# Low parts of decoded weights: ScalarE writes the negated high part and an accumulating GpSimd transfer adds the decoded block, in place of a VectorE subtraction

## Chip, cores and metric

The kernel runs on one core of one Trainium2 chip. The metric is device time in microseconds. Each execution of a kernel gives one time, and the median over the executions is compared. One more execution is recorded by the hardware profiler; its span, its groups of instructions and its waits are what this text reads.

## What is computed

Sink-and-window attention for 4 batches and 8 heads of 768 tokens, followed by a feed-forward block on the joined heads. The two matrices of the feed-forward block arrive as 64-bit floats, read as pairs of 32-bit words.

```python
def _attn_ref(q, k, v, n_sink, window):
    scores = np.matmul(q, k.transpose(0, 1, 3, 2)) / np.sqrt(64)
    keep = is_sink | in_window            # first 4 keys, or the last 128
    a = softmax(np.where(keep, scores, -1e9))
    return np.matmul(a, v)                # (4, 8, 768, 64)

def _moe_ref(x, w_in, w_out):             # x: 3072 x 512, w_in: 512 x 2048
    h = x @ w_in
    g = np.where(h >= 1, h, np.where(h <= -1, 0.0, (h + 1) ** 2 / 4))
    return g @ w_out
```

## The kernel before

**Two parts for every operand.** TensorE multiplies fp32r operands, which keep fewer bits than fp32. So an operand is written as a high part (its value rounded to fp32r) and a low part (the value less the high part), and each product is three matmuls: high by high, high by low, low by high. `w_i[j]` and `w_o[j]` hold both parts of block `j` of the two weight matrices, `t[:, 0]` the high and `t[:, 1]` the low one, each 128 x 512. There are 16 blocks of each matrix, so 32 blocks to decode, numbered `n` = 0 to 31, alternating between `w_in` and `w_out`.

**Decoding.** `weights(n)` loads the raw words of block `n` and of up to three blocks ahead (512 KB each, tile `raw`, shown as `w<-w_in` and `w<-w_out`, the first eight from SyncE's queue and the rest from ScalarE's) and calls `decode`. Three VectorE instructions (L153, L154, L155) shift and join the two words into the fp32 value in the scratch tile `w` (128 x 512). ScalarE rounds it into `t[:, 0]` (L156), and VectorE subtracts that from the value into `t[:, 1]` (L157). The scratch tile is called `o` in the profile, because it comes from a pool of two buffers under that name (pool `moe`, `bufs=2`); block `n` therefore writes the buffer that block `n-2` used.

**Stages.** 64 units of attention (a batch, a head and half the tokens, three score tiles each) form eight chunks of eight units. Beside chunk 0 stand the first 6 decode steps. Beside chunk 1 stand decode steps 6 to 27 and the first half of the feed-forward for chunk 0's rows (blocks 0 to 7). Beside chunk 2 stand the last four decode steps and the whole feed-forward of the next rows. After that no weights are decoded. Each score tile has one L243 on VectorE (mask and row maximum), whose exponential is L246 on ScalarE; each unit has one L251 on GpSimd and one L252 on VectorE, which prepare the normalisation (L264 on ScalarE and L266 on VectorE in the first 16 units). Tiles are counted by their L243: tile 12 ends unit 4, tile 36 ends unit 12 and tile 60 ends unit 20. In the profiled execution their L243 start at 22.42, 67.54 and 127.90 us.

**Order.** TensorE's order is the order of the program text (`spread` interleaves the steps by their weights). On the other engines a scheduler orders the instructions, so an added or removed instruction can move others. Each engine and each queue runs its instructions in the order given; an instruction that waits holds everything behind it on its engine.

Of the kernel before, what the change touches and what calls it, by code (L numbers as in the profile page):

```python
# [8 lines left out]
F32 = mybir.dt.float32  # L9
# [3 lines left out]
AF = mybir.ActivationFunctionType  # L13
ALU = mybir.AluOpType
# [38 lines left out]
def attn_ffn(ctx, tc, qk, vx, vs, par, w_in, w_out, out):  # L53
    nc = tc.nc
# [96 lines left out]
    def decode(t, w, words):  # L151
        low, x = words[:, :, 0], words[:, :, 1]
        nc.vector.tensor_scalar(w, x, 3, 0x3FFFFFFF, op0=ALU.logical_shift_left, op1=ALU.bitwise_and)  # L153
        nc.vector.scalar_tensor_tensor(w, x, -0x40000000, w, op0=ALU.bitwise_and, op1=ALU.bitwise_or)  # L154
        nc.vector.scalar_tensor_tensor(w, low, 29, w, op0=ALU.logical_shift_right, op1=ALU.bitwise_or)  # L155
        nc.scalar.copy(t[:, 0], w.bitcast(F32))  # L156
        nc.vector.tensor_tensor(t[:, 1], w.bitcast(F32), t[:, 0].bitcast(F32), op=ALU.subtract)  # L157

    top = {}

    def weights(n):
        def f():
            j, i = n // 2, n % 2
            for k in range(n, min(n + min(AHEAD, NJ - n // 2 - 1) + 1, 2 * NJ)):
                if k not in raw:
                    raw[k] = wpool.tile([P, 2 * DM], I32, name="w")
                    (nc.sync if k < SYNC else nc.scalar).dma_start(raw[k], (w_in, w_out)[k % 2][k // 2].bitcast(I32))
            words = raw[n].rearrange("p (c two) -> p c two", two=2)
            if i:
                w_o[j] = wpool.tile([P, 2, DM], F32R, name="w")  # L170
            decode((w_i, w_o)[i][j], moe.tile([P, DM], I32, name="o"), words)
        return f
# [440 lines left out]
    with tc.If(other_v > 0):  # L613
        with tc.tile_pool(name="gen", bufs=1) as gen:

            for n in range(2 * NJ):
                words = gen.tile([P, DM, 2], I32, name="words")
                nc.sync.dma_start(words.rearrange("p c two -> p (c two)"), (w_in, w_out)[n % 2][n // 2].bitcast(I32))
                xf = words[:, :, 1].bitcast(F32)
                m = gen.tile([P, DM], F32, name="m")  # L620
                nc.vector.tensor_tensor(m, xf, xf, op=ALU.mult)
                nc.vector.scalar_tensor_tensor(xf, m, TINY2, xf, op0=ALU.is_ge, op1=ALU.mult)
                decode((w_i, w_o)[n % 2][n // 2], m.bitcast(I32), words)
            for t0 in (0, CT):
                keep = gen.tile([P, CT, S], F32, name="keep")
                kidx = gen.tile([P, S], I32, name="kidx")
                r = gen.tile([P, S], F32, name="r")
                for i in range(CT):
                    m = keep[:, i]
                    nc.gpsimd.iota(kidx, pattern=[[-1, S]], base=(t0 + i) * P, channel_multiplier=1)  # L630
                    nc.vector.tensor_copy(r, kidx)
                    nc.vector.tensor_scalar(m, r, w_f, None, op0=ALU.is_lt)
                    nc.vector.scalar_tensor_tensor(m, r, 0.0, m, op0=ALU.is_ge, op1=ALU.mult)
                    nc.gpsimd.iota(kidx, pattern=[[1, S]], base=0, channel_multiplier=0)
                    nc.vector.tensor_copy(r, kidx)
                    nc.vector.scalar_tensor_tensor(m, r, n_f, m, op0=ALU.is_lt, op1=ALU.max)
                    nc.vector.tensor_scalar(m, m, 0.125, None, op0=ALU.mult)
                for b in range(B):
                    for h in range(H):
                        general(gen, keep, b, h, t0)  # L640
                    tail = []
                    for _, f in moe_steps(b * S + t0 * P, tail) + tail:
                        f()
# [37 lines left out]
```

## Time and profile before

| | before |
|---|---|
| median of 3 runs | 736.66 us (735.27 to 738.84) |
| profiled execution | 737.31 us, span 735.5 us, mean granted clock 0.988 |
| TensorE matmuls | 696.8 us busy (95%) |
| VectorE | 528.7 us (72%) |
| ScalarE | 507.0 us (69%) |
| GpSimd | 307.2 us (42%) |
| DMA moved | 77.79 MB, mean 106 GB/s |

The profiled execution lasted 737.31 us, which is 0.65 us over the median; it is 1.8 us longer than its span. The shares are averages over two different stages. Up to about 150 us weights are loaded and decoded beside the attention of the first chunks. After that only attention and the feed-forward remain. A row with a line number names the source line; `o<-w,o` means that a tile named `o` is written from tiles named `w` and `o`. PE is TensorE, DVE is VectorE, ACT is ScalarE, POOL is GpSimd and SP is SyncE.

### The profile page before, as it was taken

Reading aid. Unit: us, or ns where it says so; the run is one execution under the profiler, and the core shown is the slowest. Engines: PE = TensorE matmul, PEld = TensorE weight load, DVE = VectorE, ACT = ScalarE, POOL = GpSimd, SP = SyncE. Lnnn points to the kernel's source line nnn. Section 1 sums busy time; section 2 is a strip of 40 time slices with the busy share of each in tenths; the row PEclk is TensorE's granted clock in tenths of the full one; section 3 lists DMA queues with packets and bytes.
Section 4 is the critical chain, followed back from the end, with each engine's and each line's share of the span. In section 5 each row is a group of like instructions: output and inputs, shape, how many; then the busy total and the mean of one; then the engine's idle time right before and its main releaser. Section 6 shows DMA issues by size and latency. Waiting matters only on the chain.

```text
span 735.5 us, 12356 instructions
## 1 busy us (share of the span) xinstructions
PE 696.8 (95%) x3841; PEld 615.7 (84%) x3841; DVE 528.7 (72%) x1396; ACT 507.0 (69%) x1313; POOL 307.2 (42%) x537
## 2 busy tenths in 40 slices
PE   5669889899999999999999999999999999999996
PEld 3337678789999999999979998899889999989995
DVE  8999996987655666568777887877887777742221
ACT  4888797776576665578767876778767776645342
POOL 3112166554346434236554555645666454500000
PEclk9989999999999999999999999999999999999998
DMA  8987543312131311134423542324334342101001
GB/s 268 327 268 255 170 115 96 99 46 54 42 100 45 100 40 58 34 119 128 124 81 117 156 121 85 116 73 156 124 114 119 103 131 85 66 2 44 0 1 47
DMA packets 48265, 77.79 MB, mean 106 GB/s; under 512 B 13632, under 2 KB 32064, under 8 KB 48192
## 3 DMA queue, kind: packets, MB, share of 16 engines
q1 hardware_dynamic: 44736, 64.34, 28.9%
q10 hardware_dynamic: 3456, 12.58, 4.8%
q8 instruction: 32, 0.52, 0.3%
q14 instruction: 41, 0.34, 0.2%
HBM read 69.83 MB, written 7.08 MB: 105 GB/s over the span
## 4 chain that ended last, share of the span: by engine, by line
PE 64%; DVE 17%; ACT 7%; DMA 7%; issue 2%; POOL 2%; SPq 0%; ACTq 0%; POOLq 0%; DVEq 0%
PE o_ps L458 28%; PE h_ps L439 27%; PE ps_a L402 4%; DMA w<-w_in 4%; PE ps_a L239 3%; ACT p L246 2%; DVE p L266 2%; DVE k_s L223 1%; DVE o L154 1%; PE ps_a L334 1%; DVE o L155 1%; DVE p L258 1%; DVE gl L450 1%; DVE p L243 1%; DVE o L153 1%
## 5 line engine op out<-in xcount | busy, mean ns | idle before, releaser
L439 PE MATMUL h_ps<-x,wi 128*128 128x384 f32 x1536 | 308.7, 340 | 0.4 <-DVE x L480 0.4
L439 PEld LDWEIGHTS h_ps<-x,wi 128*128 128x128 f32 x1536 | 263.5, 188 | 9.3 <-DVE x L480 0.7
L458 PE MATMUL o_ps<-w,gh 128*128 128x512 f32 x768 | 244.6, 399 | 0.0
L458 PE MATMUL o_ps<-w,gl 128*128 128x512 f32 x384 | 151.3, 394 | 0.0
L458 PEld LDWEIGHTS o_ps<-w,gh 128*128 128x128 f32 x768 | 135.2, 189 | 15.7 <-issue 0.3
L446 ACT ACTIVATE g<-h_ps,half 128x384 f32<-128x384 f32 x128 | 73.9, 578 | 69.7 <-PE h_ps L439 67.7
L448 DVE SCALAR_TENSOR_TENSOR g<-g,h_ps 128x384 f32<-128x384 f32 x128 | 70.2, 549 | 68.6 <-ACT g L447 68.0
L246 ACT ACTIVATE p<-p,peak 128x260 f32<-128x260 f32 (+1 forms) x192 | 93.9, 489 | 33.9 <-DVE peak L243 32.0
L225 POOL TENSOR_TENSOR q_l<-r,q_h 128x384 fp32r<-128x384 f32 x48 | 50.3, 1047 | 142.5 <-ACT q_h L224 141.6
L449 ACT CAST gh<-g 128x384 fp32r<-128x384 f32 x128 | 65.5, 512 | 56.9 <-DVE g L448 55.9
L243 DVE CUSTOM_DVE_ANT_0 p<-ps_a,m 128x260 f32<-128x260 f32 (+1 forms) x176 | 68.5, 398 | 31.8 <-PE ps_a L239 30.5
L239 PE MATMUL ps_a<-k_s,q_h 128*128 128x260 f32 (+1 forms) x240 | 71.2, 345 | 18.6 <-DMA k_s<-qk 6.1
L458 PEld LDWEIGHTS o_ps<-w,gl 128*128 128x128 f32 x384 | 72.3, 188 | 17.5
L450 DVE TENSOR_TENSOR gl<-g,gh 128x384 fp32r<-128x384 f32 x112 | 68.0, 607 | 24.5 <-ACT gh L449 23.6
L223 DVE TENSOR_TENSOR k_s<-k_r,k_s 64x524 fp32r<-64x524 f32 (+1 forms) x44 | 45.4, 1032 | 40.9 <-ACT k_s L221 40.9
L239 PEld LDWEIGHTS ps_a<-k_s,q_h 128*128 128x128 f32 x240 | 45.2, 203 | 33.3 <-issue 10.9
L447 ACT ACTIVATE g<-g 128x384 f32<-128x384 f32 x128 | 67.0, 523 | 2.7
L346 POOL TENSOR_SCALAR_AFFINE_SELECT pt<-pt 128x384 fp32r<-128x384 f32 (+1 forms) x96 | 50.8, 530 | 24.2 <-DVE pt L339 21.7
L266 DVE TENSOR_SCALAR p<-p,stat 128x132 f32<-128x132 f32 (+1 forms) x160 | 59.1, 418 | 0.3
L344 POOL TENSOR_SCALAR_AFFINE_SELECT pt<-pt 128x384 fp32r<-128x384 f32 (+1 forms) x96 | 52.5, 547 | 8.9 <-ACT pt L338 3.9
L251 POOL TENSOR_SCALAR stat<-stat 128x3 f32<-128x3 f32 x64 | 28.6, 447 | 62.2 <-ACT p L246 53.8
L402 PEld LDWEIGHTS ps_a<-pt,v_s 128*128 128x128 f32 x304 | 46.5, 189 | 2.0
(117 smaller groups left out, 955.3 us busy)
## 6 DMA issues: line engine op xcount, KB each, us to landing
r<-qk SPq DMA_DIRECT2D x48, 192.0 KB
k_r<-qk SPq DMA_DIRECT2D x32, 262.0 KB
again<-w_in SPq DMA_DIRECT2D x16, 512.0 KB
again<-w_out SPq DMA_DIRECT2D x16, 512.0 KB
w<-w_in ACTq DMA_DIRECT2D x12, 512.0 KB
w<-w_out ACTq DMA_DIRECT2D x12, 512.0 KB
out<-o SPq DMA_DIRECT2D x23, 256.0 KB
r<-vx SPq DMA_DIRECT2D x32, 128.0 KB
```

Source lines behind the costliest of these rows:

```text
L239: nc.tensor.matmul(ps[:, lo:260], lhsT=q[:, i * P:(i + 1) * P], rhs=k_s[:, c0:c0 + 260 - lo], start=(j == 0), stop=(j == len(qs) - 1))
L243: nc.vector.tensor_tensor_reduce(out=p[:, i, lo:260], in0=ps[:, lo:260], in1=m, scale=-0.0625 if units.index(u) < NATIVE else -0.125, scal ...
L246: nc.scalar.activation(p[:, i, lo:260], p[:, i, lo:260], AF.Exp, bias=peak_i, scale=-1.0, accum_out=stat[:, i:i + 1])
L266: (nc.gpsimd if eng == "p" else nc.vector).tensor_scalar(p[:, i, lo:260], p[:, i, lo:260], r, None, op0=ALU.mult)
L402: nc.tensor.matmul(z, lhsT=w, rhs=y, start=(n == 0), stop=(n == len(mms) - 1))
L439: nc.tensor.matmul(h_ps[:, :T], lhsT=w_i[j][:, w, ct * P:(ct + 1) * P], rhs=x[:, y, ct], start=(ct == 0 and n == 0), stop=(ct == NCT - 1 a ...
L446: nc.scalar.activation(g, h_ps[:, :T], AF.Relu, bias=half, scale=0.5)
L447: nc.scalar.activation(g, g, AF.Square)
L448: nc.vector.scalar_tensor_tensor(g, g, 1.0, h_ps[:, :T], op0=ALU.min, op1=ALU.max)
L449: nc.scalar.copy(gh, g)
L450: (nc.gpsimd if row0 == GL_POOL else nc.vector).tensor_tensor(gl, g, gh.bitcast(F32), op=ALU.subtract)
L458: nc.tensor.matmul(o_ps[tt], lhsT=gg[:, tt * P:(tt + 1) * P], rhs=w_o[j][:, w], start=(j == js[0] and n == 0), stop=(j == js[-1] and n == 2))
```

## The change

The subtraction on VectorE is replaced by two steps. ScalarE writes the negated high part into `t[:, 1]`: it copies the value times -1 with the same rounding. Then a transfer issued from GpSimd's queue reads the fp32 value from the scratch tile and adds it onto `t[:, 1]` in place, which leaves the value less its high part.

```diff
         nc.scalar.copy(t[:, 0], w.bitcast(F32))
-        nc.vector.tensor_tensor(t[:, 1], w.bitcast(F32), t[:, 0].bitcast(F32), op=ALU.subtract)
+        nc.scalar.activation(t[:, 1], w.bitcast(F32), AF.Copy, scale=-1.0)
+        nc.gpsimd.dma_start(t[:, 1].bitcast(F32), w.bitcast(F32), accum_op=ALU.add)
```

Below line 157 all line numbers of the changed kernel are one higher: L243 becomes L244, L251 becomes L252. TensorE's order in the part that runs here is the same in both kernels. On VectorE the scheduler moves the decode steps. The first excerpt is from VectorE just after blocks 0 and 1 have been put together, in the kernel before; the numbers behind the names tell buffers apart (`o_358` belongs to block 2, `o_442` to block 3).

```order
L252 RECIPROCAL stat_232<-stat_232 128x3
L157 TENSOR_TENSOR wi0_151<-o_204,wi0_151 128x512
L266 TENSOR_SCALAR p_231<-p_231,stat_232 128x128
L153 TENSOR_SCALAR o_358<-w_200 128x512
L157 TENSOR_TENSOR w_289<-o_290,w_289 128x512
L154 SCALAR_TENSOR_TENSOR o_358<-w_200,o_358 128x512
L243 ISA p_268,peak_97<-ps_a_270,m0_109 128x128
```

Block 2 starts ahead of unit 3's first tile (the last row), two rows after block 0's buffer was last read. In the changed kernel block 2 (`o_360`) starts after all three tiles of units 3 and 4, directly ahead of block 3 (`o_445`), and each L153 waits for the transfer that reads the buffer's earlier content; this is VectorE again, at that later place.

```order
L244 ISA p_317,peak_97<-ps_a_327,m2_106 128x260
L253 RECIPROCAL stat_318<-stat_318 128x3
L267 TENSOR_SCALAR p_317<-p_317,stat_318 128x128
L153 TENSOR_SCALAR o_360<-w_200 128x512
L154 SCALAR_TENSOR_TENSOR o_360<-w_200,o_360 128x512
L153 TENSOR_SCALAR o_445<-w_202 128x512
L155 SCALAR_TENSOR_TENSOR o_360<-w_200,o_360 128x512
L481 TENSOR_TENSOR x0_181<-xn_169,x0_181 128x384
L154 SCALAR_TENSOR_TENSOR o_445<-w_202,o_445 128x512
```

What moved is the whole decoding: the L153 of block 2 from behind tile 6 to behind tile 12, that of block 13 from behind tile 24 to behind tile 36, and that of block 27 from behind tile 46 to behind tile 60. On GpSimd, which had no transfer of its own, the changed kernel has one between the normalisation steps for each block; these are its rows at blocks 0 to 2.

```order
L252 TENSOR_SCALAR stat_233<-stat_233 128x3
L158 DMA wi0_151<-o_204 128x512
L158 DMA w_290<-o_291 128x512
L252 TENSOR_SCALAR stat_270<-stat_270 128x3
L252 TENSOR_SCALAR stat_318<-stat_318 128x3
L284 MEMSET v_s_407 128x128
L299 TENSOR_TENSOR vsx0_137<-vs_r_1343,vsx0_137 44x64
L158 DMA wi1_152<-o_360 128x512
```

Each of these transfers stands ahead of the next unit's L252, which VectorE's reciprocal needs.

## Prediction

> **What bounds the kernel now.** I read the stages first, cut at the places the order names: tiles 12, 36 and 60 (22.4, 67.5 and 128 us). The columns are busy time of each engine, the granted clock of TensorE, and the share of the 16 DMA engines in use.
>
> ```profile
> core 0: us, PE busy (x) PEld busy (x) DVE busy (x) ACT busy (x) POOL busy (x), PEclk, DMA share, GB/s
> 9.00:22.40 13.40, 9.73 (x33) 5.42 (x34) 13.28 (x43) 10.78 (x35) 1.49 (x3) 1.00 0.97 308
> 22.40:67.50 45.10, 34.90 (x188) 22.75 (x186) 44.05 (x129) 38.27 (x116) 4.88 (x14) 0.89 0.83 282
> 67.50:128.00 60.50, 55.69 (x326) 45.90 (x325) 52.53 (x137) 49.48 (x141) 30.04 (x41) 0.97 0.46 140
> 128.00:150.00 22.00, 18.43 (x103) 15.69 (x102) 21.48 (x51) 14.24 (x40) 11.36 (x18) 1.00 0.32 91
> 150.00:300.00 150.00, 150.00 (x841) 137.45 (x841) 96.70 (x270) 101.08 (x262) 66.26 (x117) 1.00 0.21 60
> ```
>
> From 150 us TensorE is busy without a break and the change touches nothing there. So the change is worth what it does ahead of 150 us, and since TensorE's order is unchanged, each microsecond by which tile 60 comes later or earlier passes to the end. Until tile 36 VectorE is full (44.05 of 45.10 us), with ScalarE at 85% and the DMA engines at 83 to 97%. From tile 36 to 60 TensorE leads (55.69 of 60.50).
>
> Next the groups of the decode steps, and the chain that ended last, with the spacing of instructions on VectorE and the landings of weight loads (start, length, what; a DMA piece runs from its issue to its landing).
>
> ```profile
> L155 DVE SCALAR_TENSOR_TENSOR o<-w,o 128x512 int32<-128x512 int32 x32 | 23.7, 741 | 0.1
> L154 DVE SCALAR_TENSOR_TENSOR o<-w,o 128x512 int32<-128x512 int32 x32 | 23.2, 725 | 0.2
> L153 DVE TENSOR_SCALAR o<-w 128x512 int32<-128x512 int32 x32 | 14.7, 460 | 0.7 <-DVE stat L252 0.3 <-DMA w<-w_in 0.2
> L157 DVE TENSOR_TENSOR w<-o,w 128x512 fp32r<-128x512 f32 x16 | 11.8, 737 | 0.9 <-ACT w L156 0.9
> L157 DVE TENSOR_TENSOR wi<-o,wi 128x512 fp32r<-128x512 f32 x16 | 11.8, 736 | 0.0
> L156 ACT CAST w<-o 128x512 fp32r<-128x512 f32 x16 | 9.8, 614 | 1.6 <-DVE o L155 1.4
> L156 ACT CAST wi<-o 128x512 fp32r<-128x512 f32 x16 | 9.8, 611 | 6.3 <-DVE o L155 6.3
> ```
>
> ```profile
> 4.07 7.47 DMA w<-w_in
> ...
> 14.94 0.34 DVE o L153
> ...
> 17.03 0.60 DVE o L155
> 17.63 0.34 DVE p L243
> ...
> 17.97 0.60 DVE o L154
> ...
> 18.92 0.60 DVE wi L157
> ...
> 20.55 6.94 DMA w<-w_in
> ```
>
> ```profile
> 33.11 4.06 DMA w<-w_in
> ...
> 62.45 5.08 DMA w<-w_in
> ```
>
> ```profile
> 122.49 1.02 POOL q_l L225
> ...
> 125.48 2.02 DMA part<-o
> ...
> 138.02 3.44 DMA w<-w_out
> ```
>
> The reader sees that one L157 holds VectorE for 0.60 us, that a 512 KB load lands after 6.9 to 7.5 us while the DMA engines are 97% busy, after 4.1 to 5.1 us at 83%, and after 3.4 us when they are at a third.
>
> **Removed.** 32 x 0.60 = 19.2 us of VectorE. Of these 14 run between tiles 12 and 36; there 14 x 0.60 = 8.4 us go, and since four blocks less are decoded in that stretch afterwards (11 instead of 15), another 4 x (0.34 + 0.60 + 0.60) = 6.2 us. VectorE falls from 44.05 to about 29.5 us of that stage and is no bound there any more.
>
> **Added on ScalarE.** 32 copies of the size of L156. The two following rows show what one holds the engine for: the next instruction starts 0.50 us later.
>
> ```profile
> 13.30 0.60 ACT L156 CAST wi<-o 128x512 fp32r<-128x512 f32 x1
> 13.80 0.36 ACT L327 COPY pt<-ps_a 128x256 f32<-128x256 f32 x1
> ```
>
> I take 0.53 us each (between that spacing and the 0.61 of its length), 17 us in all. Between tiles 12 and 36: 38.27 - 15 x 0.53 + 11 x 2 x 0.53 = 42.0 us. Between 36 and 60 (10 casts now, 13 blocks later): 49.48 - 5.3 + 13.8 = 58.0 us. These are floors, since ScalarE would have to run without a pause. So VectorE's relief cannot be worth more than 45.1 - 42.0 = 3.1 us and 60.5 - 58.0 = 2.5 us in these stages. Ahead of tile 12, blocks 2 and 3 leave VectorE, and ScalarE's 10.78 us would bound it: at most 13.40 - 10.78 = 2.6 us. From 128 to 150 us, where VectorE is full (21.48 of 22 us), three L157 go, 1.8 us. Together 10.0 us is the most that can be won.
>
> **Added on GpSimd and the DMA engines.** 32 transfers, each reading a 256 KB block and the 256 KB it is added to. GpSimd is idle for most of this time (4.88 of 45.10 us), but a transfer waits there for its negated copy, and L251 of the next unit stands behind it, and behind that the reciprocal on VectorE. The trace has neither a transfer from GpSimd nor an accumulating one. From below: 2.0 us, the 256 KB `part<-o` with half-idle engines. From above: 7.5 us, the 512 KB load ahead of tile 12, with 1.05 us for GpSimd's issue (as long as one L225, 1.02) where SyncE's costs 0.43 of the load's time: 8.1 us. Two rows are near: traffic of 512 KB is that of a weight load, so I take the loads' landings of the same stage. For tiles 12 to 36 the rows are 6.94, 4.06 and 5.08, at a DMA share of 0.83. The transfers raise that share: 11 x 0.5 MB = 5.8 MB at 282 GB/s / 0.83 = 340 GB/s are 17 us of 45, or half of that if only the block itself counts, 0.19 to 0.38 more. The engines are then as full as ahead of tile 12, so I take that stage's rows, 7.2 us (7.47 and 6.94). For tiles 36 to 60, 14 transfers bring 0.46 to about 0.8; there 4.06 and 5.08 apply, 4.6 us.
>
> The Trainium skill, "DMA: Bandwidth & Descriptors", section on the anatomy of a transfer from GpSimd, fits one as 2.0 us plus its bytes over 436 GB/s, an estimate of 2.6 us for 256 KB and 3.2 us for 512 KB. The 2.02 us row agrees, the 6.94 us row of the busy stage doesn't; by it the transfer would be hidden, which is the first rival's case.
>
> **The wait that it makes.** Before, a scratch buffer was free when L157 had read it, and L153 of block n+2 never waited for it. Now it is free when the transfer of block n has landed, and that L153 stands on VectorE with the attention's rows behind it. One turn of a buffer: L153, L154, L155 with about one tile's row between them, 0.34 + 0.60 + 0.60 + 0.4 = 2.0 us (rounded up); 0.5 us until ScalarE takes it up (the rows below: L155 ends its hold at 23.37, L156 starts at 24.17; in other places 0.1); cast and negated copy 0.50 + 0.61 = 1.1 us; then the transfer, T. That is 3.6 us + T for two blocks.
>
> ```profile
> 22.77 0.68 DVE L155 SCALAR_TENSOR_TENSOR o<-w,o 128x512 int32<-128x512 int32 x1
> 23.37 0.42 DVE L153 TENSOR_SCALAR o<-w 128x512 int32<-128x512 int32 x1
> ```
>
> ```profile
> 24.17 0.60 ACT L156 CAST wi<-o 128x512 fp32r<-128x512 f32 x1
> ```
>
> What the places in the order allow: blocks 2 to 13 lie between tiles 12 and 36, 11 steps in 45.1 us, 4.1 us each, a turn of 8.2 us, so T up to 4.6 us is hidden. Blocks 13 to 27 lie between tiles 36 and 60, 14 steps in 60.5 us, a turn of 8.6 us, T up to 5.0 us. The first is exceeded: 3.6 + 7.2 = 10.8 us a turn, 5.4 us a block, 11 x 5.4 = 59.4 us where 45.1 stood, +14.3 us. The second is not: 3.6 + 4.6 = 8.2 us. Ahead of tile 12 block 2's buffer is awaited from about 14.4 (both copies of block 0) + 7.2 = 21.6 us, just before tile 12, so little is won there. The matmuls themselves don't wait for weights: their blocks 0 to 7 are used beside decode steps 6 to 27.
>
> **Sum.** On the profiled execution of 737.3 us: -19.2 us of VectorE, of which nothing ends up at the end because the waits take its place, +17 us of ScalarE beside those waits, +14.3 us of waiting between tiles 12 and 36, 0 after tile 36. That gives 751.6 us; the median of the runs is 0.65 us below that execution, so 751 us.
>
> Ends of the range. Below, T is hidden everywhere and ScalarE runs without a pause: 737.3 - 10.0 = 727. Above, T = 8.1 us everywhere: a turn of 11.7 us, 11 x 5.85 - 45.1 = +19.3 us and 14 x 5.85 - 60.5 = +21.4 us, 778 us.
>
> **Rivals.**
> (1) The transfer is hidden, T below 4.6 us throughout. For it: GpSimd is idle, nothing reads HBM in these transfers, and the 2.02 us and 3.44 us rows. Against it: 83 to 97% busy DMA engines. VectorE's relief then counts, limited by ScalarE. It was 80 to 85% busy in its best stages and would have to be 93 to 96% busy; I give half the floors' gain, 5 us: 732 us.
> (2) Gains and losses cancel: T between about 4.6 and 5.5 us early, so that 11 x (3.6 + 5.5) / 2 = 50 us costs 5 us, against up to 5 us won ahead of tile 12 and after tile 36. 737 us, within 0.5% of before. That is about the least change that a measurement of this kernel can tell from none.
> (3) The transfer is slower than any row: GpSimd is held from building it. L153 (128 x 512 in 0.42 us) runs faster than L154 (0.68 us), so VectorE works there in another mode. The Trainium skill, "SBUF — State Buffer", in its box on SBUF's two sides, says that GpSimd cannot write a transfer's descriptors while VectorE runs in a mode that takes both ports; no transfer here can show it yet. Were each transfer held for one L153, 0.42 us, that adds 0.2 us to each of 25 steps, 5 us; were it held so often that T passes 8.1 us, the time passes 778 us, some 790 us at T = 9: 11 x 6.3 + 14 x 6.3 - 105.6 = +52 us.
>
> **Chances.** Forecast case (T between 5.5 and 8.1 us early, 741 to 778 us) 0.54; rival 1 0.17; rival 2 0.16; rival 3 0.13. So faster by over 0.5% 0.17, within it 0.16, slower 0.67. The range 730 to 779 leaves out rival 3 and the better part of rival 1's own spread (727 to 730). The forecast case alone has 741 to 778.
>
> **What would show it.** GpSimd has 32 transfer rows, VectorE loses 23.6 us of L157, ScalarE gains 17 to 20 us. L153 should show idle time ahead of it that a transfer ends, about 14 us more or less between tiles 12 and 36; tile 36 should come at about 81 us and tile 60 at 142 us; after that nothing differs. The prediction is wrong if L153 finds its buffer free (T under 4.6 us), if waits gather after tile 36, if a normalisation step on GpSimd, held behind a transfer, becomes what VectorE waits for, or if ScalarE sets the pace instead.

## The result and the profile after

The changed kernel takes 793.25 us (median of 4 runs, 790.52 to 797.29) against 735.96 us before (four runs now, with the three that gave 736.66), a ratio of 1.0777 with a 95% interval of [1.0736, 1.0818]. It is slower by 57.3 us. The prediction had the sign, but its 751 us and its range to 779 us are too low. The profiled execution has a span of 788.6 us, 53.1 us more than before.

First the groups of the decode steps of the changed kernel (busy time, mean ns | idle time of the engine just ahead, and what ended it). L157 is now ScalarE's negated copy and L158 the transfer; "part" is a partial output of the feed-forward on its way to memory.

```profile
L158 POOL DMA_DIRECT2D wi<-o x16 | 14.6, 911 | 51.7 <-issue 21.1 <-ACT p L247 7.2 <-ACT g L447 5.1
L158 POOL DMA_DIRECT2D w<-o x16 | 14.5, 907 | 40.3 <-DVE o L155 11.0 <-issue 10.7 <-ACT w L157 5.8
L153 DVE TENSOR_SCALAR o<-w 128x512 int32<-128x512 int32 x32 | 14.0, 437 | 45.8 <-DMA w<-o 19.8 <-DMA part<-o 9.8 <-DMA wi<-o 9.5
L253 DVE RECIPROCAL stat<-stat 128x3 f32<-128x3 f32 x64 | 10.9, 171 | 13.0 <-POOL stat L252 11.3
L157 ACT ACTIVATE w<-o 128x512 fp32r<-128x512 f32 x16 | 10.0, 626 | 0.0
```

The 45.8 us of idle time ahead of L153 were 0.7 us before. A transfer ended 29.3 us of it (19.8 and 9.5), and a partial output that held a buffer of the same pool ended 9.8 us. New as well is GpSimd's own idle time under "issue" (time in which it waits for nothing that the profile shows), 31.8 us in 9 gaps, each just ahead of a transfer, and the reciprocal waits 11.3 us for GpSimd's L252, where it waited 0.3 us in the kernel before:

```profile
L252 DVE RECIPROCAL stat<-stat 128x3 f32<-128x3 f32 x64 | 10.9, 170 | 2.4 <-POOL stat L251 0.3
```

The stages, cut as in the prediction at tiles 12, 36 and 60, and the stretch from tile 60 to 63 (columns as there):

```profile
core 0: us, PE busy (x) PEld busy (x) DVE busy (x) ACT busy (x) POOL busy (x), PEclk, DMA share, GB/s
9.00:23.50 14.50, 8.31 (x30) 4.97 (x30) 7.24 (x30) 10.08 (x33) 3.32 (x5) 1.00 1.04 335
23.50:85.30 61.80, 40.88 (x183) 28.60 (x183) 31.84 (x103) 42.50 (x126) 12.71 (x24) 0.75 0.74 195
85.30:162.40 77.10, 62.48 (x336) 50.54 (x335) 54.88 (x138) 55.70 (x151) 42.59 (x54) 0.89 0.68 175
162.40:188.70 26.30, 12.09 (x50) 10.39 (x49) 14.57 (x36) 13.18 (x32) 10.06 (x15) 0.68 0.53 137
```

No compute engine is full in any of them: the stages are made of waits. From tile 72 to the end both kernels take the same 565.8 us, so the whole loss lies ahead of it:

| from tile to tile | before, us | after, us | loss | predicted |
|---|---|---|---|---|
| start to 12 | 22.42 | 23.52 | 1.1 | about 0 |
| 12 to 36 | 45.1 | 61.8 | 16.7 | 14.3 |
| 36 to 60 | 60.4 | 77.1 | 16.8 | 0 |
| 60 to 63 | 13.1 | 26.2 | 13.2 | 0 |
| 63 to 72 | 28.7 | 34.1 | 5.4 | 0 |

How a wait comes about can be followed at blocks 2 and 3. VectorE of the changed kernel (start, length; L153 begins a block and L155 ends it):

```profile
26.15 0.42 DVE L153 TENSOR_SCALAR o<-w 128x512 int32<-128x512 int32 x1
27.23 0.43 DVE L153 TENSOR_SCALAR o<-w 128x512 int32<-128x512 int32 x1
...
30.42 0.69 DVE L155 SCALAR_TENSOR_TENSOR o<-w,o 128x512 int32<-128x512 int32 x1
...
36.25 0.43 DVE L153 TENSOR_SCALAR o<-w 128x512 int32<-128x512 int32 x1 [3.73 <-DMA wi<-o]
...
40.70 0.43 DVE L153 TENSOR_SCALAR o<-w 128x512 int32<-128x512 int32 x1 [0.82 <-DMA w<-o]
...
183.63 0.43 DVE L153 TENSOR_SCALAR o<-w 128x512 int32<-128x512 int32 x1 [8.84 <-DMA part<-o]
```

and its transfers on GpSimd, for blocks 0 to 3, with two pieces of the chain of waits (a DMA piece runs from issue to landing):

```profile
14.44 1.04 POOL L158 DMA_DIRECT2D wi<-o  x1 [0.81 <-ACT pt L328]
21.02 0.90 POOL L158 DMA_DIRECT2D w<-o  x1 [5.54 <-issue]
...
29.81 0.91 POOL L158 DMA_DIRECT2D wi<-o  x1 [1.38 <-DVE peak L244]
...
36.55 0.92 POOL L158 DMA_DIRECT2D w<-o  x1 [4.63 <-issue]
```

```profile
15.48 5.52 issue
...
29.81 6.42 DMA wi<-o
36.25 0.44 DVE o L153
```

Block 2 behaves as the prediction said: its transfer is issued at 29.81 and lands at 36.23, and L153 of block 4 starts at 36.25. Block 3 does not. VectorE has put it together at 31.1 and ScalarE's copies follow until 32.99, but its transfer starts only at 36.55, when block 2's has landed. GpSimd does nothing for 4.63 us, and after 32.99 nothing that the trace names is missing. The whole run looks like this: no transfer starts before the one ahead of it has landed, and 16 of the 31 start within 0.5 us of that landing, more than the 9 gaps under "issue".

In the later stage other rows stand between those of one block. This is VectorE at block 27, whose part lasts from 166.22 to 169.54:

```profile
166.22 0.59 DVE L153 TENSOR_SCALAR o<-w 128x512 int32<-128x512 int32 x1 [1.28 <-DMA w<-o]
...
167.16 0.52 DVE L449 SCALAR_TENSOR_TENSOR g<-g,h_ps 128x384 f32<-128x384 f32 x1
167.60 0.68 DVE L154 SCALAR_TENSOR_TENSOR o<-w,o 128x512 int32<-128x512 int32 x1
168.20 0.73 DVE L267 TENSOR_SCALAR p<-p,stat 128x128 f32<-128x128 f32 x3
168.86 0.68 DVE L155 SCALAR_TENSOR_TENSOR o<-w,o 128x512 int32<-128x512 int32 x1
```

From the starts of the five rows of each block, the mean turn of a buffer is:

| | VectorE's three rows | to ScalarE | two copies | GpSimd's delay | transfer to next L153 | turn | allowed |
|---|---|---|---|---|---|---|---|
| predicted, blocks 2 to 12 | 2.0 | 0.5 | 1.1 | 0 | 7.2 | 10.8 | 8.2 |
| measured | 2.85 | 0.35 | 1.18 | 2.01 | 4.77 | 11.2 | |
| predicted, blocks 13 to 26 | 2.0 | 0.5 | 1.1 | 0 | 4.6 | 8.2 | 8.6 |
| measured | 3.61 | 0.44 | 1.18 | 1.68 | 4.69 | 11.6 | |

So the transfer itself was sized too high early and right late (over all 32, from issue to landing, 3.3 us at the least, 4.1 in the middle, 7.4 at the most). What was missing is GpSimd's delay and VectorE's longer part. The longer part could have been read in the kernel before. There the time from the start of L153 to the end of L155 is 3.1 us on the mean for blocks 2 to 12 and 3.4 us for blocks 13 to 26, and still 2.6 and 3.0 us without the 0.60 us of each L157 in between. This is block 14 in it (other rows left out):

```profile
50.88 0.42 DVE L153 TENSOR_SCALAR o<-w 128x512 int32<-128x512 int32 x1
...
51.56 0.69 DVE L157 TENSOR_TENSOR w<-o,w 128x512 fp32r<-128x512 f32 x1
...
52.37 0.69 DVE L154 SCALAR_TENSOR_TENSOR o<-w,o 128x512 int32<-128x512 int32 x1
...
53.75 0.66 DVE L155 SCALAR_TENSOR_TENSOR o<-w,o 128x512 int32<-128x512 int32 x1
```

The experiments ask what the delay is, what the accumulating costs, whether the two buffers are the cause, and whether there was a gain to be had at all.

### The profile page after: what moved, and what is told of

It is laid out like the page before. It is cut to its first block, busy times and chain, and to the rows that moved or that the text cites. A ratio compares the mean times of both kernels' runs of the same rounds, so it can differ in the third digit from the quotient of the medians.

```text
span 788.6 us, 12457 instructions
## 1 busy us (share of the span) xinstructions
PE 712.0 (90%) x3841; PEld 629.4 (80%) x3841; DVE 514.9 (65%) x1364; ACT 524.0 (66%) x1345; POOL 334.8 (42%) x569
## 3 DMA queue, kind: packets, MB, share of 16 engines
q0 software_dynamic: 4608, 8.39, 6.2%
## 4 chain that ended last, share of the span: by engine, by line
PE 63%; DVE 15%; DMA 7%; issue 6%; ACT 6%; POOL 3%; SPq 0%; ACTq 0%; POOLq 0%; DVEq 0%
PE o_ps L459 26%; PE h_ps L440 26%; PE ps_a L240 4%; PE ps_a L403 4%; DVE p L267 2%; DMA wi<-o 2%; ACT p L247 2%; PE ps_a L335 2%; DVE o L154 1%; DVE p L259 1%; DVE k_s L224 1%; DVE o L155 1%; PE ps_a L368 1%; DVE gl L451 1%; DMA w<-o 1%
## 5 line engine op out<-in xcount | busy, mean ns | idle before, releaser
L440 PE MATMUL h_ps<-x,wi 128*128 128x384 f32 x1536 | 314.2, 344 | 3.9 <-DVE x L481 3.2
L440 PEld LDWEIGHTS h_ps<-x,wi 128*128 128x128 f32 x1536 | 268.0, 191 | 13.2 <-DVE x L481 3.5
L459 PE MATMUL o_ps<-w,gh 128*128 128x512 f32 x768 | 247.8, 404 | 14.2 <-ACT o L465 14.2
L459 PE MATMUL o_ps<-w,gl 128*128 128x512 f32 x384 | 153.5, 400 | 4.5 <-POOL gl L451 4.5
L240 PE MATMUL ps_a<-k_s,q_h 128*128 128x260 f32 (+1 forms) x240 | 73.6, 356 | 25.8 <-DVE sk L342 7.1
L244 DVE CUSTOM_DVE_ANT_0 p<-ps_a,m 128x260 f32<-128x260 f32 (+1 forms) x176 | 68.3, 399 | 35.7 <-PE ps_a L240 34.5
L240 PEld LDWEIGHTS ps_a<-k_s,q_h 128*128 128x128 f32 x240 | 48.0, 215 | 38.7 <-issue 10.2
L347 POOL TENSOR_SCALAR_AFFINE_SELECT pt<-pt 128x384 fp32r<-128x384 f32 (+1 forms) x96 | 49.8, 520 | 24.2 <-DVE pt L340 21.6
L345 POOL TENSOR_SCALAR_AFFINE_SELECT pt<-pt 128x384 fp32r<-128x384 f32 (+1 forms) x96 | 51.9, 542 | 7.8 <-ACT pt L339 3.8
L403 PE MATMUL ps_a<-pt,v_s 128*128 128x256 f32 (+1 forms) x304 | 47.0, 275 | 0.0
```

The costliest lines, as they stand in the source:

```text
L240: nc.tensor.matmul(ps[:, lo:260], lhsT=q[:, i * P:(i + 1) * P], rhs=k_s[:, c0:c0 + 260 - lo], start=(j == 0), stop=(j == len(qs) - 1))
L244: nc.vector.tensor_tensor_reduce(out=p[:, i, lo:260], in0=ps[:, lo:260], in1=m, scale=-0.0625 if units.index(u) < NATIVE else -0.125, scal ...
L403: nc.tensor.matmul(z, lhsT=w, rhs=y, start=(n == 0), stop=(n == len(mms) - 1))
L440: nc.tensor.matmul(h_ps[:, :T], lhsT=w_i[j][:, w, ct * P:(ct + 1) * P], rhs=x[:, y, ct], start=(ct == 0 and n == 0), stop=(ct == NCT - 1 a ...
L459: nc.tensor.matmul(o_ps[tt], lhsT=gg[:, tt * P:(tt + 1) * P], rhs=w_o[j][:, w], start=(j == js[0] and n == 0), stop=(j == js[-1] and n == 2))
```

## Experiments

Each diff is against the changed kernel unless said otherwise. Differences are against the runs of the kernel before on the same chip (735.96, 737.72 or 736.59 us).

### Room for the descriptors of GpSimd's transfers

The number is what the program sets aside for descriptors (explained below), in bytes a partition.

```diff
-num_devices=1, dynamic_dma_scratch_size=512)
+num_devices=1, dynamic_dma_scratch_size=1024)
```

> The changed kernel with 1024 instead of 512 bytes a partition for the descriptors of GpSimd's transfers; every engine's order is the same. Theory A (a second transfer cannot be written while the first is in flight, so GpSimd stands still until it has landed): the idle time put down to issue ahead of the transfers on GpSimd, 31.8 us, falls below 5 us, and the time falls by 20 to 40 us, to 753 to 773 us. Theory B (two scratch buffers: the L153 of block n+2 waits for the landing of block n whatever GpSimd does): GpSimd's idle time falls, but L153 still waits about 30 us for landings, and the time stays within 8 us of 793 us. Theory C (landings are slow because the DMA engines are full and an accumulating transfer reads twice): no change, 788 to 797 us.

784.34 us, ratio 1.064 [1.0608, 1.0671]: +48.4 us, 8.9 us less than the changed kernel. The order on every engine is the same as there. GpSimd's rows for blocks 0 and 1, and the largest wait between 9 and 210 us (us in total, times, longest):

```profile
14.41 1.04 POOL L158 DMA_DIRECT2D wi<-o  x1 [0.81 <-ACT pt L328]
15.86 0.87 POOL L158 DMA_DIRECT2D w<-o  x1 [0.40 <-ACT w L157]
```

```profile
DVE o L153 <- DMA w<-o: 24.5, 9, 6.4
```

The second transfer now starts at 15.86, as soon as its copy is written, where it started at 21.02. Idle time under "issue" ahead of a transfer is gone. Of the 31 later transfers 13 now start while the one ahead is still on its way. So the standstill was room: with 512 bytes the second transfer did not start until the first had landed. The Trainium skill, "DMA: Bandwidth & Descriptors", section "SWDGE vs HWDGE vs iDMA", says that GpSimd writes such a transfer's descriptors, the orders to the DMA engines, into rings in a reserved part of SBUF, which the DMA engines drain. No trace shows the rings themselves; the two runs fit them, with 31.8 us of standstill at 512 bytes and none at 1024. While GpSimd stands still, its other work stands with it.

Of the 31.8 us of standstill only 8.9 come back, by the medians; the profiled executions differ by 4.8 us. The gain lies ahead of tile 36, which comes 6.7 us earlier; from there to tile 60 this run takes 80.0 us, against 77.1. The time lies between what theories A and B expected. The turn is 10.9 us early and 11.6 late: two transfers now run at once, and from issue to the next L153 takes 6.2 us and 5.8 us where it took 4.8 and 4.7.

### A plain copy in place of the accumulating transfer

```diff
-nc.gpsimd.dma_start(t[:, 1].bitcast(F32), w.bitcast(F32), accum_op=ALU.add)
+nc.gpsimd.dma_start(t[:, 1].bitcast(F32), w.bitcast(F32))
```

> The changed kernel with a plain copy of the decoded block over the low part in place of the accumulating transfer, from the same queue, in the same order on every engine (so the low parts hold the whole value; only the time is read). Theory C (the second read of the accumulating transfer): landings fall from a median of 4.1 us to about 2.5 us and the time falls by 15 to 35 us. Theory A: if a copy takes fewer descriptors, two fit at once, GpSimd's issue idle falls below 10 us and the time falls as in the run with more descriptor space, to 753 to 773 us; if it takes as many, nothing changes. Theory B: it falls only as far as the landings get shorter, 5 to 15 us.

770.23 us, ratio 1.0468 [1.0445, 1.0491]: +34.3 us, in the order of the changed kernel and with its 512 bytes. The queue of GpSimd's transfers (packets, MB, share of the 16 engines' span), first in the changed kernel, then in this one:

```profile
q0 software_dynamic: 4608, 8.39, 6.2%
```

```profile
q0 software_dynamic: 2560, 8.39, 2.8%
```

```profile
L158 POOL DMA_DIRECT2D wi<-o x16: 536/584/756, 14.9 to 173.4; - x16
...
DMA to landing us min/median/max: 2.3/4.0/6.9
```

For the same bytes the accumulating form takes 4608 / 32 = 144 packets each, nine for each DMA engine, against five, and 6.2% of 788.6 us = 48.9 us of all 16 engines, 1.5 us a block, against 2.8% of 769.1 = 21.5 us, 0.67 us a block. GpSimd builds it in 0.91 us against 0.58. With the smaller form no idle time under "issue" is left in the same room either. The Trainium skill, "Collectives: The Full Stack", section "The bandwidth ceiling", says that a DMA addition costs two source reads and two read descriptors for each piece; the nine packets against five, and 2.3 times the engine time, agree in kind, though no trace here shows the reads themselves.

Against the doubled room, which has no standstill either, the accumulating form costs 784.3 - 770.2 = 14.1 us. Half of it lies early: tiles 12 to 36 take 51.2 us here and 58.2 there. From 36 to 60 the plain copy still takes 76.5 us, and a turn 11.0 us, against 77.1 and 11.6 us in the changed kernel: there the form and the room together are worth little. L153 waits 4.9 us for landings in that stage here and 12.2 us in the changed kernel, and yet the stage is only 0.6 us shorter. So those waits alone do not set its length. No run keeps this order of VectorE's rows without a transfer, so what the order costs by itself stays open.

### Six scratch buffers, with and without the room

```diff
+            if n == 0:
+                scratch.append(xpool.tile([P, 6, DM], I32, name="x"))
+            w = scratch[0][:, n % 6] if n < WMID else moe.tile([P, DM], I32, name="o")
-            decode((w_i, w_o)[i][j], moe.tile([P, DM], I32, name="o"), words)
+            decode((w_i, w_o)[i][j], w, words)
```

Not shown is the line `scratch = []` above it; `WMID` is 28.

> The changed kernel with six scratch buffers for blocks 0 to 27 (in space that the second input tile takes only afterwards), not shared with the feed-forward's outputs; blocks 28 to 31 keep the two old ones. The scheduler then puts the decode steps about as early as in the kernel before (block 13 behind tile 21, block 27 behind tile 40). Theory B (buffers): L153's waits of 29 us for landings and of 9.8 us for the partial outputs disappear and the time falls to 735 to 755 us. Theory A: GpSimd's standstill stays, about 5 us for every transfer beside the attention's steps queued there, and through it the reciprocal on VectorE waits: 765 to 793 us.

798.33 us, ratio 1.0855 [1.0836, 1.0875]: no better than two buffers, and above both expectations. Its largest waits between 9 and 210 us:

```profile
DVE stat L257 <- POOL stat L256: 68.5, 11, 13.8
ACT p L269 <- DVE stat L257: 55.2, 9, 11.3
...
POOL w L158 <- issue: 23.8, 6, 6.8
POOL wi L158 <- issue: 22.3, 5, 7.3
```

More transfers are ready at once, and they queue on GpSimd for room (25 of the 31 start within 0.5 us of the landing ahead of them), and the unit's L256 (the L252 of the changed kernel) stands behind them, with the reciprocal, the normalisation and TensorE after it: tiles 12 to 36 take 89.2 us. With both changed together:

> Six scratch buffers for blocks 0 to 27 and twice the descriptor space; the order is that of the run with six buffers alone. If A and B together are the loss, no wait for a transfer is left on VectorE or GpSimd before tile 60, and only the added work of ScalarE (17 us, on an engine 80 to 85% busy) and the relief of VectorE count: 728 to 742 us. If C (full DMA engines delay the loads of weights, keys and queries) matters beside them, TensorE waits for loads and the time stays above 745 us.

755.99 us, ratio 1.0284 [1.0263, 1.0306]: 28.4 us less than the room alone and 42.3 us less than the buffers alone. So two buffers and the room are two limits in a row, and either hides what the other is worth. Two of its stages, and two pieces of its chain:

```profile
24.60:58.00 33.40, 18.21 (x80) 11.92 (x79) 21.06 (x62) 23.55 (x68) 10.60 (x17) 0.67 1.07 296
...
117.00:147.00 30.00, 29.61 (x184) 25.42 (x183) 17.98 (x61) 23.21 (x70) 17.71 (x28) 1.00 0.26 75
```

```profile
19.16 12.01 DMA w<-w_out
...
31.64 13.96 DMA v_s<-vx
```

The late stage is short again: tiles 36 to 60 take 56.8 us, against 60.4 before, in part because the decoding now comes earlier (block 27 behind tile 40). The early one takes 65.3 us against 45.1, which is the whole loss of 20.0, with the DMA engines full (1.07) and loads of weights and heads that need 12 and 14 us. Two controls show what of that belongs to the transfers. The kernel before with the same six buffers (diff as above, against the kernel before):

> The kernel before with six scratch buffers for blocks 0 to 27 and nothing else changed. It shows what the buffers do without a transfer: the blocks come earlier (block 13 behind tile 18 instead of 24, block 27 behind tile 35 instead of 46), and with them the weight loads. If the earlier loads crowd out those of keys and queries, 740 to 746 us, and that much of the 756.0 us of six buffers with transfers is not the transfers'. If not, 734 to 739 us.

749.95 us, ratio 1.0199 [1.017, 1.0229]: the buffers alone, with no transfer in the kernel, cost 13.4 us, more than the 740 to 746 us expected. The scheduler then decodes earlier (block 27 behind tile 33, not 46), and tiles 12 to 36 take 58.7 us. And the plain copy with six buffers and the room:

> Six scratch buffers and twice the descriptor space, with a plain copy in place of the accumulating transfer, in the same order (the low parts hold the whole value; only the time is read). With buffers and descriptors out of the way the DMA engines were full up to 117 us. If the accumulating transfers' own time on the engines is what is left of the loss (756.0 us against 736.0), the copy takes about half of that time and the time falls to 740 to 748 us. If the weight loads, which come earlier in this order, are what crowds out the rest, it stays at 752 to 757 us.

743.62 us, ratio 1.0087 [1.0052, 1.0122]. So 14 of the 20.0 us of the accumulating version go with its form (20.0 less 5.9, the same as with two buffers). What is left, 5.9 us, is less than the 13.4 us of the kernel before with six buffers. That kernel has yet another order (block 13 behind tile 18, not 21), so the rest is not divided further here.

### Is there a gain to be had?

The transfer left out, ScalarE's negated copy kept:

```diff
-nc.gpsimd.dma_start(t[:, 1].bitcast(F32), w.bitcast(F32), accum_op=ALU.add)
```

> The changed kernel without the transfer: ScalarE writes the negated high part and nothing is added to it (the low parts are left out of the result). The scratch buffer is free when ScalarE has read it; the scheduler puts the blocks early (block 13 behind tile 19, block 27 behind tile 35). If all of the loss comes from the transfers, what is left is VectorE's relief against ScalarE's extra work: 727 to 738 us. If ScalarE's 17 us are part of the loss, or the earlier weight loads crowd out the loads of keys and queries, 742 us or more.

736.99 us, ratio 0.9992 [0.9975, 1.0009]. Its stage from 22 to 66 us:

```profile
22.00:66.00 44.00, 31.30 (x153) 20.11 (x154) 40.97 (x112) 43.84 (x124) 4.62 (x13) 0.77 0.90 316
```

ScalarE is busy for 43.84 of 44.0 us there, VectorE for 40.97. Without a transfer the scheduler decodes earlier (block 27 behind tile 35, not 46), so tiles 12 to 36 take 8.8 us more than before and tiles 36 to 60 take 6.8 us less. In this order, then, VectorE's relief is worth nothing even with a transfer that costs nothing, and ScalarE is full where the decoding lies. An order that spreads the decoding out was not tried. What ScalarE's part costs shows when VectorE adds the block onto the negated copy, so that VectorE does as much as before, in nearly the order of before:

```diff
-nc.gpsimd.dma_start(t[:, 1].bitcast(F32), w.bitcast(F32), accum_op=ALU.add)
+nc.vector.tensor_tensor(t[:, 1], w.bitcast(F32), t[:, 1].bitcast(F32), op=ALU.add)
```

> ScalarE writes the negated high part and VectorE adds the decoded block to it, so VectorE has its instruction back and ScalarE has 32 more than the kernel before: the price of ScalarE's part alone. If ScalarE has room where it stands (85% busy up to tile 36), 736 to 740 us; if its 17 us stand in the way, 742 to 752 us.

743.35 us, ratio 1.0089 [1.0061, 1.0118]: +5.6 us for 32 copies. The run without the transfer, which leaves out these 32 additions, is 6.4 us shorter. So the relief seems worth about as much as ScalarE's part costs. This is argued and not shown, since the orders differ too (block 27 behind tile 35 there and tile 45 here).

Both VectorE and ScalarE without the low part, which GpSimd clears instead:

```diff
-nc.scalar.activation(t[:, 1], w.bitcast(F32), AF.Copy, scale=-1.0)
-nc.gpsimd.dma_start(t[:, 1].bitcast(F32), w.bitcast(F32), accum_op=ALU.add)
+nc.gpsimd.memset(t[:, 1].bitcast(F32), 0.0)
```

> The kernel before without the subtraction and without a transfer or a negated copy: GpSimd clears the low parts, so that they are left out of the result. It shows what the relief of VectorE alone is worth. The negated copy cost 5.6 us by itself and negated copy and relief together nothing; so the relief is worth about 5 us and this run takes 728 to 733 us. If ahead of 150 us the loads or TensorE set the pace instead, 734 to 738 us.

740.58 us, ratio 1.0054 [1.0035, 1.0073]. This one does not answer its question: the scheduler moved many of the clears to the start of the program, and tile 12 came 10.4 us late (more in the last section). Behind tile 12, tiles 12 to 60 take 100.4 us against 105.5, 5.1 us less. That is near the relief above, but some of it may be work that ran ahead during those 10.4 us; no run separates the two.

The subtraction on GpSimd in place of both:

```diff
-nc.scalar.activation(t[:, 1], w.bitcast(F32), AF.Copy, scale=-1.0)
-nc.gpsimd.dma_start(t[:, 1].bitcast(F32), w.bitcast(F32), accum_op=ALU.add)
+nc.gpsimd.tensor_tensor(t[:, 1], w.bitcast(F32), t[:, 0].bitcast(F32), op=ALU.subtract)
```

> The kernel before with the subtraction of L157 on GpSimd instead of VectorE: VectorE is relieved of the same 19 us, with no transfer, no wait for a landing and nothing more on ScalarE; GpSimd gets 32 subtractions of about 1.4 us (its 128 x 384 ones take 1.05). If VectorE up to tile 36 is worth anything, 726 to 734 us. If the two engines hold each other up (VectorE's rows are up to 1.5 us long where GpSimd works beside them), 735 to 742 us.

747.96 us, ratio 1.0154 [1.0117, 1.0191]. Its groups of subtractions:

```profile
L157 POOL TENSOR_TENSOR wi<-o,wi 128x512 fp32r<-128x512 f32 x16 | 22.6, 1411 | 16.4 <-ACT wi L156 16.2
L157 POOL TENSOR_TENSOR w<-o,w 128x512 fp32r<-128x512 f32 x16 | 21.9, 1368 | 7.7 <-ACT w L156 7.5
```

1.4 us on GpSimd holds a buffer for far less than a turn with a transfer, and the loss is 10.2 us instead of 57.3. That is still more than either case that was expected, and where it arises was not followed. No version here beats the kernel before.

### Which blocks lose it

The late blocks stay as before in the first of these two; in the second the condition is `n >= 14`, and the early ones do. `decode` is given the block's number `n`; those lines are not shown.

```diff
+        if not (n < 14):
+            nc.vector.tensor_tensor(t[:, 1], w.bitcast(F32), t[:, 0].bitcast(F32), op=ALU.subtract)
+            return
```

> Negated copy and transfer for blocks 0 to 13 only; blocks 14 to 31 have the subtraction on VectorE as before. By the prediction's own split nearly all of the loss arises up to tile 36, with these blocks: this run would show it alone, 750 us or more, and the run with the late blocks alone about 737 us. By the changed kernel's trace, where a turn of a scratch buffer took 11.2 us for blocks 2 to 12 and 11.6 us for blocks 13 to 26, each half costs its own share: 750 to 758 us here.

> Negated copy and transfer for blocks 14 to 31 only; blocks 0 to 13 have the subtraction on VectorE as before. By the prediction (a turn of 8.2 us, which tiles 36 to 60 allow) 735 to 741 us. If it was the turn that was sized too small (VectorE's part 3.6 us instead of 2.0, GpSimd's standstill of 1.7 us left out), these blocks cost about the 17 us lost between tiles 36 and 60 and the 13 us between tiles 60 and 63, where the buffers are shared with the partial outputs: 758 to 775 us.

764.2 us (+27.6), ratio 1.0387 [1.0345, 1.0428], with the transfers for blocks 0 to 13 alone; 765.7 us (+29.1), ratio 1.0417 [1.0379, 1.0455], for blocks 14 to 31 alone. The sum, 56.7, is the whole loss of 57.3. Late blocks cost as much as early ones, which the prediction had at nothing. The totals add up, but the stages do not. The stage from tile 36 to 60, first with the early blocks alone, then with the late ones alone:

```profile
84.70:156.50 71.80, 59.70 (x342) 48.16 (x341) 66.05 (x159) 52.87 (x148) 37.12 (x44) 0.95 0.52 157
```

```profile
70.80:156.10 85.30, 62.66 (x332) 50.29 (x331) 50.33 (x130) 57.48 (x156) 37.84 (x53) 0.86 0.58 148
```

One of the waits with the late blocks alone, between 70 and 190 us (L161 is the transfer there):

```profile
POOL wi L161 <- issue: 10.5, 2, 6.1
```

With the early blocks alone the stage takes 71.8 us where 60.4 stood, 11.4 us of that run's 27.6, though only the transfers of blocks 12 and 13 are left in it. The decoding comes late there (block 27 behind tile 57, not 46), and VectorE is busy for 66.05 of 71.8 us. So blocks that are held up early seem to crowd the stage behind as well. With the late blocks alone it takes 85.3 us, with the DMA engines at 58%: it is not their load that makes the turn long, and GpSimd stands still for lack of room here too (10.5 us in two gaps). The tiles 60 to 63 take 12.0 us in this kernel and 12.8 in the other, not 26.2. So the 18.6 us that the changed kernel loses between tiles 60 and 72 are not a fixed cost of the last four blocks, whose transfers the second version has too.

## Why the prediction was wrong

- **Sign and the wait named, right.** L153 waits for the transfer that reads its buffer, and the lost time ahead of tile 72 passes to the end whole. With six buffers and room for the descriptors 37 us of the 57 go.
- **32 transfers on GpSimd, ScalarE +17 us, tile 36 at 81 us: near.** ScalarE's busy time rose from 507.0 to 524.0 us, the lower end. Tile 36 came at 85.3 us. The early term, +14.3 us, measured +16.7.
- **The early term is right in size by luck: two errors cancel.** The step "the engines are then as full as ahead of tile 12, so I take that stage's rows, 7.2 us" failed: the DMA share there was 0.74, less than the 0.83 before (195 GB/s instead of 282: the loads are spread over a longer time), and the transfer took 4.8 us. In its place stand 2.0 us of delay on GpSimd, which the prediction put at nothing, and 0.85 us more of VectorE. With the doubled room that delay is 0.4 us, so most of it was standstill.
- **The late term failed: "the second is not: 3.6 + 4.6 = 8.2 us".** T of 4.6 was right (4.7). The 3.6 us was not: VectorE's part took 3.6 us instead of 2.0 (2.7 in the middle; blocks 25 and 26 took 7.7 and 6.4), since in that stage rows of the attention and the feed-forward stand between L153 and L155, as at block 27; with 0.4 and 1.2 us for ScalarE's part it is 5.2. The delay on GpSimd added 1.7. The turn is 11.6 us against 8.6 allowed: 14 blocks at 5.8 us are 81 us, and the L153 of blocks 13 and 27 stand 80.0 us apart. With a margin of 0.4 us in 8.6, the 2.0 us, used for both stages, had to hold to a fifth of its size. The kernel before has 3.0 for these blocks, and with it the prediction's own sum is 9.2 us against 8.6 allowed, a loss and not a margin. The rest of the late loss is only in part explained: without the standstill the delay is 0.5 us and the turn still 11.6, since the transfers then overlap and each takes longer, and with the early blocks alone the stage loses 11.4 us nearly without transfers.
- **"After tile 36 nothing" failed by 35.4 us:** 16.8 to tile 60 and 18.6 behind it. The largest wait of L153 there is 8.84 us, for a partial output in the pool it shares. The prediction counted the scratch buffers as if they were the decoding's alone. Why this is 13 us here and nothing in the two half versions stays open.
- **GpSimd's normalisation step held behind a transfer,** named as what would make it wrong, happened: the reciprocal's wait for it rose from 0.3 to 11.3 us here and to 68.5 us with six buffers.
- **Rival 3** named the place, GpSimd held from building its transfers, and a time near the measured one. Its mechanism was another: a VectorE mode, and T past 8.1 us. The transfers never took more than 7.4 us, and the hold went with twice the room, with VectorE's rows in the same order. So it was room, and the nearness of the time was luck.
- **Rivals 1 and 2** had gains of up to 5 us. The fastest transfer took 3.3 us, above both estimates of 2.6 and 3.2 us that the prediction worked out. Without the transfer the kernel is even with the one before: no run here came near 732 us.

## What to carry to other kernels

When a step becomes a chain over more engines, add up the turn of its buffer over all of them, in each stage with that stage's rows, and count who else uses the pool; a margin of a few tenths of a microsecond is none. A transfer from GpSimd is an instruction on GpSimd as well: look at what stands behind it there, and at the room for its descriptors, since without it the engine stands still under "issue". Before moving work off the fullest engine, read how full the engine that takes it would be: here it was full up to tile 36 even without the transfer, and the best version measured was no change.

## What was not expected of the hardware

- An accumulating transfer of 128 x 512 fp32 within SBUF takes as much as all 16 DMA engines for 1.5 us, and GpSimd for 0.91 us, 2.3 and 1.6 times a plain copy of the same bytes. With 512 bytes of descriptor room the next one waited for its landing; with 1024 two were in the air at once, and three at once with six buffers.
- TensorE was granted less clock in the stages where it lost time: 0.75 between tiles 12 and 36, where it was 0.89, and 0.68 between tiles 60 and 63. Waiting alone does not make it so: ahead of tile 12 it was busy for 8.31 of 14.50 us at 1.00. Over the run its mean fell from 0.988 to 0.954, and its busy time rose from 696.8 to 712.0 us.
- In the kernel that clears the low parts, a small row of VectorE took 5.40 us beside a stretch of clears on GpSimd that ended with it (first VectorE, then GpSimd):

```profile
5.42 5.40 DVE L81 TENSOR_SCALAR big<-par_f 128x2 f32<-128x2 f32 x1
...
13.18 1.97 DVE L115 TENSOR_SCALAR x<-x,nw 128x128 f32<-128x128 f32 x1
```

```profile
5.20 5.60 POOL L157 MEMSET wi<- 128x512 f32 x12
...
13.16 1.45 POOL L157 MEMSET wi<- 128x512 f32 x3
```

The twelve clears run from 5.20 to 10.80 and L81 from 5.42 to 10.82. In the kernel before L81 takes 0.16 us. The row behind it, L82, came 5.7 us later than there. L115 took 1.97 us beside the next clears, where it takes 0.28. The Trainium skill, "SBUF — State Buffer", section "SBUF: two separate sides", says that the pair of ports that VectorE, in some of its modes, shares with GpSimd is an exclusive lock, held for the whole instruction. The 5.40 us fit such a lock if twelve clears in a row had it before VectorE did. No trace shows the lock itself, and no run here separates it from another cause.
